# SyncE's wait ahead of a key unit's load: from ScalarE's copy and the last direct product to the first product read from the copy

## The chip, the cores and the metric

The kernel runs on one core of a Trainium2 chip. Its time is the device time of one execution in microseconds (us). Before the change the median of three runs is 694.32 us (693.97 to 694.38). A profile of one execution shows what each engine and the DMA did within its span; that execution took 693.89 us in all, 692.1 us of it the span.

## The reference

One decode step of a gated mix of two blocks, for a single token x of 512 numbers, all in float32:

```python
q = (x @ wq)                       # 32 heads of 128; 8 key/value heads, 4 query heads share one
scores = einsum("bhqd,bhkd->bhqk", q, k) * (Dh ** -0.5)
p = softmax(scores, axis=-1)       # over 32768 cached positions
a = einsum("bhqk,bhkd->bhqd", p, v) @ wo
b = (silu(x @ w1) * (x @ w3)) @ w2 # the MLP, 1792 wide
g = sigmoid((x * gate_w).sum(-1))
return g * a + (1 - g) * b
```

The key cache and the value cache are 8 x 32768 x 128 float32 each, 134 MB apiece. Nearly all bytes that the kernel reads are these two.

## The kernel before, in words

**Units.** The key cache is read in 16 units of 128 partitions x 16384 float32 (8.4 MB), four units to a window of two key/value heads. The value cache is read in 16 units of the same size. A unit's number is called t for keys; values run four units behind keys (`LAG = 4`).

**Buffers.** Two large SBUF buffers hold one unit each: `big_a` and `big_b` (keys `A0`, `A1`, `B0`, `B1` for their halves, called regions z = 0 and z = 1). Key units 0 and 2 go into `big_b`, units 1 and 3 into `big_a`; after these the MLP weights w1 and w3 and then the value units use `big_b`, and every later key unit goes into `big_a`. So from unit 4 on a key unit's load has to wait until the unit before it has been read out of `big_a`.

**Reading a key unit.** `set_aside` (L318) lets ScalarE copy three quarters of region z = 1 into a third buffer, `aside`, so that the large buffer comes free sooner. `scores` works in eight parts, (z, c) with z = 0, 1 and c = 0 to 3. For each part VectorE transposes 128 x 2048 numbers into one of two small buffers (L346; `kt`, of which one lies beside `aside` and bears that name in the profile), and TensorE multiplies the result with the query window (L330, `scores_part`). The parts (0, 0) to (0, 3) and (1, 0) are read from the large buffer itself, and (1, 1), (1, 2), (1, 3) from ScalarE's copy. Unit 3 is an exception: its part (1, 0) is copied as well (L320, into `extra`, a free corner of `big_b`), so that `big_a` is read by z = 0 and ScalarE alone, and a one-element VectorE copy `mark2` (L352) marks the end of the transposes of z = 0.

**Values.** `load_values` (L413) loads a value unit into `big_b` once TensorE has finished the products of the previous one (`values_all`, L432).

**What sets the order.** Each engine has its own list of operations, written in program order. `Program.add` works out the waits: an operation that writes a buffer waits for the buffer's writer and readers on other engines. VectorE's transposes hand over to TensorE by a semaphore that is counted down (a credit) and so have no running count of their own; whoever depends on one waits instead for the TensorE product that took the credit (`via`), a count on the semaphore `PE`. A wait that is implied by another one is left out: each operation carries the counts known to be reached when it is done (`after`). An operation with two waits gets a separate wait instruction first (L110) and has the second on the instruction itself.

SyncE issues all large loads through one queue (q1), in this order in the steady part: key unit, value unit, key unit, value unit. Before the change a key unit's load waits for two counts: ScalarE's, for the copy of the previous unit in that buffer, and TensorE's, for its product of part (1, 0). Unit 4's load waits for ScalarE's copy to `extra` and for VectorE's mark. Unit 1's load waits for the query products.

**The steps around it.** After each fourth unit, scores are turned (L368), reduced to a maximum by VectorE (L379 to L391) and put through the exponential by ScalarE (L398). At the end come the last value units, wo and w2, outside of the loops.

Of the kernel before, what the change touches and what calls it, by code (L numbers as in the profile page):

```python
# [23 lines left out]
class Program:  # L24
# [16 lines left out]
            self.sems[name] = self.sem(name)  # L41
        return self.sems[name]

    def add(self, eng, fn, reads=(), writes=(), over=(), inc=None, by=1, credit=None, credits=(), loop=False, also=None):

        op = Op(eng, fn, credits, loop)
        clock = self.clock[eng]
        for c, _ in credits:
            for k, v in c.after.items():
                clock[k] = max(clock.get(k, 0), v)  # L50
        deps = {}
        for k in reads:
            assert k in self.writer, k
            deps[self.writer[k]] = True
        for k in (*writes, *over):
            if k in self.writer:
                deps[self.writer[k]] = True
            for r in self.readers.get(k, ()):
                deps.setdefault(r, False)
        need = {}  # L60
        taken = {c for c, _ in credits}
        for d, data in deps.items():
            if d in taken or (d.eng == eng and (eng == "PE" or not data)):
                continue
            if d.done is None:
                d = d.via
                if d is None or d.eng == eng:
                    assert d is not None
                    continue
            k, v = d.done  # L70
            if clock.get(k, 0) < v:
                need[k] = max(need.get(k, 0), v)
        for k, v in sorted(need.items(), key=lambda kv: -self.by[kv].index):
            if clock.get(k, 0) >= v:
                continue
            assert not loop, (fn, k, v)
            op.waits.append((k, v))
            for a, b in self.by[k, v].after.items():
                clock[a] = max(clock.get(a, 0), b)
        op.index = len(self.by)  # L80
        op.after = dict(clock)
        if credit:
            op.inc = (credit, by)
        elif inc is None and by == 0:
            op.inc = None
        else:
            s = inc or eng
            self.count[s] = self.count.get(s, 0) + by
            op.inc, op.done = (s, by), (s, self.count[s])
            op.after[s] = self.count[s]  # L90
            self.by[op.done] = op
        for c, _ in credits:
            c.via = op
        for k in reads:
            self.readers.setdefault(k, []).append(op)
        for k in writes:
            self.writer[k], self.readers[k] = op, []
        if also:
            self.writer[also] = op
        self.ops[eng].append(op)  # L100
        return op
# [15 lines left out]
def kernel(  # L117
# [13 lines left out]
    nc = tc.nc  # L131
# [16 lines left out]
    LAG = 4  # L148
# [12 lines left out]
    def sbuf(name, *shape):  # L161
        return nc.alloc_sbuf_tensor(name, [P, *shape], F32)[:]

    big = [sbuf("big_a", 2 * R), sbuf("big_b", 2 * R)]
# [22 lines left out]

    lanes = [0]

    def load(dst, src, writes, over=()):  # L190
        lanes[0] += 1
        lane = f"load{lanes[0] % 9}"
        return pr.add(
            "SP", lambda: nc.sync.dma_start(dst, src), writes=writes, over=[*over, lane], inc=lane, by=16, also=lane,  # L194
        )

    def region(b, z):
        return big[b][:, z * R:(z + 1) * R]
# [26 lines left out]
    for src, dst, view, axes in (  # L225
# [11 lines left out]
            reads=[src], writes=[dst])  # L237
# [6 lines left out]
    def clear(**kw):  # L244
        pe(zeros,
           reads=["acc"], writes=["s"], **kw)
# [15 lines left out]
    for c in range(NC):  # L262
# [19 lines left out]
        reads=["gate0"], writes=["gate1"])  # L282
# [4 lines left out]
    for b in range(2):  # L287
        qt = kt[b][:, 0:512]
        dve(lambda b=b, qt=qt: V.transpose(qt, rows[b]), reads=[f"row{b}"], writes=[f"kt{b}"])
        for j in range(4):  # L290
            w, u = divmod(4 * b + j, 2)
            src = qt[32 * j:32 * j + 32, :].rearrange("p (q c x) -> p x c q", q=4, c=4)[:, 0]
            for e in range(2):
                r, o = 2 * u + e, 16 + 8 * e + 4 * u
                dst = win[32 * r:32 * r + 32, w, :, o:o + 4]
# [5 lines left out]
    kd = k_cache.rearrange("a (w u) s d -> w (a u s d)", u=2).rearrange("w (p m r) -> w m p r", p=P, m=4)  # L301
    vd = v_cache.rearrange("a h (e p n) d -> (a h) e p (n d)", e=2, p=P)

    def where(t):
        return 1 if t in (0, 2) else 0

    def load_keys(t):
        b = where(t)
        load(big[b], kd[t // 4, t % 4], ["AB"[b] + str(z) for z in range(2)])

# [3 lines left out]
    def set_aside(t):  # L316
        src, key = region(where(t), 1).rearrange("p (n r) -> p n r", n=NB), "AB"[where(t)] + "1"
        act(lambda: A.copy(spare, src[:, :, 32:128]), reads=[key], writes=["wo"])  # L318
        if t == LAG - 1:
            act(lambda: A.copy(extra, src[:, :, 0:32]), reads=[key], writes=["extra"], over=["B1"])  # L320

    def window(t, z):
        return act(
            lambda: A.copy(winc, win[:, t // 4, :, 16 - 16 * z:48 - 16 * z]),  # L324
            reads=[("win", t // 4, r) for r in range(4)], writes=["winc"], credit="windows",
        )

    def scores_part(c):
        for g in range(4):
            ins = T.matmul(  # L330
                ps_s[32 * g:32 * g + 32, :], winc[:, c, :], kt[c % 2][:, 512 * g:512 * g + 512],
                start=False, stop=False, skip_group_check=True,
            )
        return ins

    def scores(t, z, win_op):
        kin = region(where(t), z).rearrange("p (n c j) -> p c n j", c=4, j=32)
        ks = []
        for c in range(4):
            src, key = kin[:, c], "AB"[where(t)] + str(z)  # L340
            if (z, c) >= (1, 1):
                src, key = spare[:, :, 32 * (c - 1):32 * (c - 1) + 32], "wo"
            elif z == 1 and t == LAG - 1:
                src, key = extra, "extra"
            dst = kt[c % 2].rearrange("p (n i) -> p n i", i=32)
            k = dve(lambda d=dst, s=src: V.transpose(d, s), reads=[key], writes=[f"kt{c % 2}"], credit="keys")  # L346
            pe(lambda c=c: scores_part(c), reads=[f"kt{c % 2}", "winc"], writes=["s"], loop=True,
               credits=((win_op, 1), (k, 1)) if c == 0 else ((k, 1),))
            ks.append(k)

        if t == LAG - 1 and z == 0:
            done = dve(lambda: V.tensor_copy(mark2, ones[:, 0:1]), reads=["ones"], writes=["mark2"])  # L352
            for k in ks:
                k.via = done

    def scores_out(t):
        o = act(
            lambda: A.copy(sb[:, :, :, t % 4], ps_s.rearrange("p (n i) -> p n i", i=32)),  # L358
            reads=["s"], writes=[("sb", t % 4)], credit="scores",
        )  # L360
        return o
# [80 lines left out]
    def own(s):  # L442
        h, e = divmod(s, 2)
        dve(lambda: V.tensor_tensor(
            tmp[:, e], ps_o.rearrange("p (b d) -> p b d", b=4), own_b.unsqueeze(2).to_broadcast([P, 4, P]), op=ALU.mult,
        ), reads=["o", "own_b"], writes=[f"tmp{e}"])
        if e == 1:
            dve(lambda: V.tensor_reduce(red[h], tmp.rearrange("p e b d -> p d (e b)"), axis=AX.X, op=ALU.add),  # L448
                reads=["tmp0", "tmp1"], writes=[("red", h)])


    def load_hidden():
        for z, t in enumerate((w1, w3)):
            load(big[1][:, z * NC * F:(z + 1) * NC * F], t.rearrange("(p c) f -> p (c f)", c=NC), [f"B{z}"])
# [28 lines left out]
    def store(e, src, key, inc):  # L483
        i, q = (0, nc.scalar) if e == "ACT" else (1, nc.sync)
        pr.add(e, lambda: q.dma_start(outs[2 * i:2 * i + 2, :], src[31 + 64 * i:33 + 64 * i, :]),
               reads=[key], writes=[("out", i)], inc=inc, by=16)

    load_keys(0)
    vals = {}
    first = window(0, 0)  # L490
    for t in range(NH):
        v = t - LAG
        set_aside(t)
        scores(t, 0, first)
        scores(t, 1, window(t, 1))
        out_op = ((scores_out(t), 1),)
        if v < 0:
            clear(loop=True, credits=out_op)
        if t == LAG - 1:
            load_hidden()  # L500
        if t + 1 < NH:
            load_keys(t + 1)
            first = window(t + 1, 0)
        if v >= 1:
            own(v - 1)
        if t % 4 == 3:
            turn(v >= 0, out_op if v >= 0 else ())
        if v >= 0:
            values_loop(vals.pop(v), weights(v), () if t % 4 == 3 else out_op)
            clear(loop=True)  # L510
        if t == LAG - 1:
            hidden_products()
        if v + 1 >= 0 and t + 1 < NH:
            vals[v + 1] = load_values(v + 1)

        if t % 4 == 3:
            softmax(t // 4)
        if t % 4 == 0 and t > 0:
            total(t // 4 - 1)
        if t == LAG:  # L520
            hidden()
# [175 lines left out]
    a, b, c, d = flips  # L697
# [67 lines left out]
```

## Time and profile before

| what | us |
|---|---|
| median of three runs | 694.32 (693.97 to 694.38) |
| the profiled execution | 693.89 |
| its span | 692.1 |
| TensorE busy | 388.3 |
| VectorE busy | 370.1 |
| ScalarE busy | 134.7 |
| SyncE's separate waits, for ScalarE's copy | 195.7, 14 of them |
| SyncE's waits for TensorE's score products | 124.2, 17 of them |

How to read the rows: the page's first part gives each engine's busy time and share of the span. A line of the table by stretches gives the stretch, its length, busy time of PE (TensorE), PEld (its weight loads), DVE (VectorE), ACT (ScalarE) and POOL (GpSimd) with instruction counts, the granted TensorE clock, the mean busy share of the 16 DMA engines, and GB/s. A line of the timeline gives start, duration, engine, line of the kernel, operation, output and input, and in square brackets the idle time before it and what ended it; SPq is SyncE's queue, and its lines are issues of transfers. A line of the waits gives who waited, for whom, the total, the count and the longest. A line of the DMA issues ends with the time from issue to landing; where it was asked for a short stretch, it is that of the one transfer issued there.

### The profile page before, as it was taken

To read this page: it belongs to the slowest core of one execution; us is meant where nothing else is said; L and a number is where in the kernel's file an instruction comes from. 1 tells how busy PE (TensorE), PEld (TensorE's weight loads), DVE (VectorE), ACT (ScalarE), POOL (GpSimd) and SP (SyncE) were. 2 spreads that over 40 slices of the span, in tenths; PEclk is the share of its full clock that TensorE was granted. 3 is DMA by queue.
4 is the path that set the end of the run, shared out by engine and by line. 5 is a ranking of instruction groups with operands and counts; after the bars stand their busy time and mean duration, and the time that the engine had idled before them with its cause. 6 is when DMAs were issued, how large, how long until landed. Compare 5 with 4: busy or idle time off the path is not lost. (4 is left out here: it accounts for less than half of the span.)

```text
span 692.1 us, 5789 instructions
## 1 busy us (share of the span) xinstructions
PE 388.3 (56%) x2448; PEld 95.3 (14%) x2448; DVE 370.1 (53%) x259; ACT 134.7 (19%) x113; POOL 2.8 (0%) x15
## 2 busy tenths in 40 slices
PE   1537677566473636565564646364563646564457
PEld 0101111201010101201010101101010101211112
DVE  1049998493725637493826537492816547600701
ACT  0143323222303131220303131220303031100000
POOL 1000000000000000000000000000000000000000
PEclk9969999968686966778695779788697879865789
DMA  9999999999999999999999999999999999999996
GB/s 394 444 432 424 428 424 432 449 439 432 424 432 424 443 447 432 428 428 428 432 443 443 428 428 428 428 443 447 432 424 428 428 436 439 421 451 425 422 429 287
DMA packets 6213, 296.35 MB, mean 428 GB/s; under 512 B 694, under 2 KB 698, under 8 KB 1084
## 3 DMA queue, kind: packets, MB, share of 16 engines
q1 hardware_dynamic: 6196, 296.23, 99.1%
q8 instruction: 6, 0.10, 0.1%
q14 instruction: 3, 0.02, 0.0%
q10 hardware_dynamic: 8, 0.01, 0.0%
HBM read 296.23 MB, written 0.00 MB: 428 GB/s over the span
## 5 line engine op out<-in xcount | busy, mean ns | idle before, releaser
L346 DVE STREAM_TRANSPOSE aside<-big_a 128x2048 f32<-128x2048 f32 x41 | 94.4, 2302 | 184.3 <-DMA big_a<-in_A_k_cache_dram 184.3
L330 PE MATMUL ps<-aside,winc 128*32 128x512 f32 x512 | 89.4, 776 | 168.0 <-PEq L703 167.2
L330 PE MATMUL ps<-kt,winc 128*32 128x512 f32 x512 | 89.0, 772 | 49.1 <-PEq L703 49.1
L318 ACT COPY aside<-big_a 128x6144 f32<-128x6144 f32 x14 | 74.4, 5313 | 171.2 <-DMA big_a<-in_A_k_cache_dram 171.2
L432 PE MATMUL ps<-big_b,pv 128*32 128x512 f32 x768 | 94.9, 650 | 17.4 <-PEq L703 17.4
L346 DVE STREAM_TRANSPOSE kt<-aside 128x2048 f32<-128x2048 f32 x32 | 72.7, 2273 | 0.0
L346 DVE STREAM_TRANSPOSE kt<-big_a 128x2048 f32<-128x2048 f32 x28 | 63.5, 2269 | 0.0
L330 PEld LDWEIGHTS ps<-aside,winc 128*32 128x32 f32 x512 | 13.1, 120 | 236.6 <-issue 236.6
L358 ACT COPY sb<-ps 128x512 f32<-128x512 f32 x16 | 17.1, 1071 | 136.5 <-PE ps L330 136.5
L432 PEld LDWEIGHTS ps<-big_b,pv 128*32 128x32 f32 x768 | 27.7, 119 | 85.0 <-issue 85.0
L346 DVE STREAM_TRANSPOSE aside<-aside 128x2048 f32<-128x2048 f32 x16 | 36.3, 2269 | 0.0
L587 PE MATMUL ps<-big_b,probs 128*32 128x512 f32 x128 | 19.1, 756 | 21.1 <-DMA big_b<-in_A_v_cache_dram 21.1
L330 PEld LDWEIGHTS ps<-kt,winc 128*32 128x32 f32 x512 | 13.1, 120 | 125.4 <-issue 125.4
L596 DVE TENSOR_SCALAR red<-ps,own_b 128x128 f32<-128x128 f32 x2 | 0.7, 350 | 52.7 <-PE ps L587 52.7
L324 ACT COPY winc<-win 128x128 f32<-128x128 f32 x32 | 9.8, 307 | 77.9 <-PE ps L330 77.9
L587 PE MATMUL ps<-big_a,probs 128*32 128x512 f32 x128 | 18.1, 730 | 7.6 <-DMA big_a<-in_A_v_cache_dram 7.6
L346 DVE STREAM_TRANSPOSE aside<-big_b 128x2048 f32<-128x2048 f32 x7 | 16.0, 2291 | 11.0 <-DMA big_b<-in_A_k_cache_dram 11.0
L641 PE MATMUL ps<-win,ones 128*128 128x512 f32 (+1 forms) x40 | 21.8, 631 | 0.0
L242 PE MATMUL ps<-acc 128*128 128x512 f32 x34 | 20.0, 670 | 2.5 <-POOL acc L213 1.5
L379 DVE TENSOR_REDUCE mt<-turned 128x8 f32<-128x2048 f32 x4 | 9.2, 2292 | 20.3 <-PE turned L368 20.3
L405 DVE TENSOR_REDUCE sums<-probs 128x8 f32<-128x2048 f32 x4 | 15.3, 3834 | 2.1 <-ACT probs L398 2.1
L268 PE MATMUL turned<-big_a,xp 128*32 128x512 f32 x64 | 8.6, 699 | 12.0 <-DMA big_a<-in_A_wq_dram 12.0
(94 smaller groups left out, 186.9 us busy)
## 6 DMA issues: line engine op xcount, KB each, us to landing
big_b<-in_A_v_cache_dram SPq DMA_DIRECT2D x2, 4096.0 KB, 25.8
big_b<-in_B_w_dram SPq DMA_DIRECT2D x2, 3584.0 KB, 20.8
aside<-in_A_wo_dram SPq DMA_DIRECT2D x1, 4096.0 KB, 29.4
big_a<-in_A_wo_dram SPq DMA_DIRECT2D x1, 4096.0 KB, 20.4
big_a<-in_B_w_dram SPq DMA_DIRECT2D x2, 1024.0 KB, 23.5
big_a<-in_B_w_dram SPq DMA_DIRECT2D x1, 768.0 KB, 26.0
big_a<-in_B_w_dram SPq DMA_DIRECT2D x1, 512.0 KB, 26.7
big_a<-in_B_w_dram SPq DMA_DIRECT2D x1, 256.0 KB, 26.9
```

The costliest lines, as they stand in the source:

```text
L242: return T.matmul(ps_s, acc[:, 0:P], acc, start=True, stop=False, skip_group_check=True)
L268: ins = T.matmul(pf[b][32 * j:32 * j + 32, :], xp[:, c, :], t[:, o:o + REP * DH], start=(c == 0), stop=(c == NC - 1),)
L318: act(lambda: A.copy(spare, src[:, :, 32:128]), reads=[key], writes=["wo"])
L324: lambda: A.copy(winc, win[:, t // 4, :, 16 - 16 * z:48 - 16 * z]),
L330: ins = T.matmul(ps_s[32 * g:32 * g + 32, :], winc[:, c, :], kt[c % 2][:, 512 * g:512 * g + 512], start=False, stop=False, skip_group_chec ...
L346: k = dve(lambda d=dst, s=src: V.transpose(d, s), reads=[key], writes=[f"kt{c % 2}"], credit="keys")
L358: lambda: A.copy(sb[:, :, :, t % 4], ps_s.rearrange("p (n i) -> p n i", i=32)),
L379: dve(lambda: V.tensor_reduce(mt[:, 0:8], turned.rearrange("p (n q) -> p q n", q=8), axis=AX.X, op=ALU.max), reads=banks, writes=["mt"])
L405: dve(lambda: V.tensor_reduce(sums[:, 8 * w:8 * w + 8].rearrange("p (u q) -> p u q", u=2), probs[:, :, 0:1024].rearrange("p u (n q) -> p u ...
L432: ins = T.matmul(ps_o[32 * t:32 * t + 32, :], pv[:, o:o + 32], big[1][:, n * P:(n + 4) * P], start=((z, g) == (0, 0)), stop=((z, g) == (1, ...
L587: ins = T.matmul(ps_o[32 * t:32 * t + 32, :], prob[u][:, o:o + 32], vt[:, n * P:(n + 4) * P], start=((e, z, g) == (0, 0, 0)), stop=((e, z, ...
L641: return T.matmul(bank[:, 0:n], ones, win.rearrange("p w c n -> p (w c n)")[:, 0:n], start=True, stop=True)
```

## The change

A key unit's load gets an added dependency, `behind`: the VectorE transpose of part (1, 1), which is the first that reads ScalarE's copy. Through `via` it becomes a wait for TensorE's product of part (1, 1). Since that transpose comes after ScalarE's copy, the wait for ScalarE is implied by it and is left out, and so is the earlier count on TensorE. Which unit's part it is: the unit that occupied the same buffer, that is the second last one for units 2 and 3 (`read[-2:-1]`) and the last one from unit 4 on (`read[-1:]`). For unit 1 the slice is empty and nothing is added. In the changed order the loads of units 2, 3 and 5 to 15 wait for TensorE alone, and unit 4's for VectorE's mark and TensorE. All engines keep their instructions and their order; loads that do not go through `load_keys` keep their waits. In the changed file the lines stand two to four further down (L194 becomes L196, L330 becomes L332, L346 becomes L348).

```diff
-    def add(self, eng, fn, ..., loop=False, also=None):
+    def add(self, eng, fn, ..., loop=False, also=None, behind=()):
...
+        for d in behind:
+            deps[d] = True
...
-    def load(dst, src, writes, over=()):
+    def load(dst, src, writes, over=(), behind=()):
...
-            "SP", lambda: nc.sync.dma_start(dst, src), writes=writes, over=[*over, lane], inc=lane, by=16, also=lane,
+            "SP", lambda: nc.sync.dma_start(dst, src), writes=writes, over=[*over, lane], inc=lane, by=16, also=lane, behind=behind,
...
-    def load_keys(t):
+    def load_keys(t, behind=()):
         b = where(t)
-        load(big[b], kd[t // 4, t % 4], ["AB"[b] + str(z) for z in range(2)])
+        load(big[b], kd[t // 4, t % 4], ["AB"[b] + str(z) for z in range(2)], behind=behind)
...
             ks.append(k)
+            if (z, c) == (1, 1):
+                read.append(k)
...
-    vals = {}
+    vals, read = {}, []
...
         if t + 1 < NH:
-            load_keys(t + 1)
+            load_keys(t + 1, read[-1:] if t + 1 >= LAG else read[-2:-1])
             first = window(t + 1, 0)
```

More of the change, by code (lines that the diff above doesn't have):

```diff
@@ L42, in semaphore, with add @@
         return self.sems[name]
-    def add(self, eng, fn, reads=(), writes=(), over=(), inc=None, by=1, credit=None, credits=(), loop=False, also=None):
+    def add(self, eng, fn, reads=(), writes=(), over=(), inc=None, by=1, credit=None, credits=(), loop=False, also=None, behind=()):
         op = Op(eng, fn, credits, loop)
```

## The prediction

> **What bounds the kernel now.** I read the busy shares and the DMA row of the page first, then the DMA shares over four long stretches, then the landings of the key units as ScalarE sees them.
>
> ```profile
> PE 388.3 (56%) x2448; PEld 95.3 (14%) x2448; DVE 370.1 (53%) x259; ACT 134.7 (19%) x113; POOL 2.8 (0%) x15
> DMA  9999999999999999999999999999999999999996
> q1 hardware_dynamic: 6196, 296.23, 99.1%
> 0.00:43.30 43.30, 11.62 (x72) 3.74 (x72) 4.39 (x13) 6.14 (x21) 2.81 (x15) 0.92 0.97 412
> 43.30:137.90 94.60, 65.05 (x376) 15.86 (x376) 77.31 (x46) 31.99 (x21) 0.00 (x0) 0.95 1.00 433
> 137.90:563.90 426.00, 236.38 (x1462) 52.50 (x1462) 237.70 (x135) 87.42 (x64) 0.00 (x0) 0.76 1.00 434
> 563.90:690.00 126.10, 75.30 (x538) 23.19 (x538) 50.69 (x65) 9.12 (x7) 0.00 (x0) 0.78 0.97 418
> 292.71 5.31 ACT L318 COPY aside<-big_a 128x6144 f32<-128x6144 f32 x1 [3.44 <-DMA big_a<-in_A_k_cache_dram]
> 331.41 5.31 ACT L318 COPY aside<-big_a 128x6144 f32<-128x6144 f32 x1 [17.94 <-DMA big_a<-in_A_k_cache_dram]
> 370.11 5.31 ACT L318 COPY aside<-big_a 128x6144 f32<-128x6144 f32 x1 [17.44 <-DMA big_a<-in_A_k_cache_dram]
> 408.81 5.31 ACT L318 COPY aside<-big_a 128x6144 f32<-128x6144 f32 x1 [17.11 <-DMA big_a<-in_A_k_cache_dram]
> 447.82 5.31 ACT L318 COPY aside<-big_a 128x6144 f32<-128x6144 f32 x1 [7.51 <-DMA big_a<-in_A_k_cache_dram]
> ```
>
> No compute engine is busy for more than 56% of the span; queue q1, on which SyncE puts every large load, fills 99.1% of the 16 DMA engines. From 43.3 to 563.9 us the DMA share is 1.00 at 433 to 434 GB/s. A key unit's landing is the moment ScalarE's copy of it starts: 292.71, 331.41, 370.11, 408.81, always 38.70 us apart, and between two lie one key and one value transfer of equal size, so 19.35 us each. (The last gap is 39.01; I return to it.) While the queue is never empty the end moves by nothing: a load issued later only waits less behind its predecessor. So the question for this change is by how much each load is issued ahead of its predecessor's landing (its lead), and what lead a load needs.
>
> **The change: what is removed.** SyncE now makes two waits ahead of a key unit's load: one on ScalarE's copy (L110, the separate instruction) and one on TensorE (on the load itself, L194).
>
> ```profile
> SPq L110 <- ACT aside L318: 195.7, 14, 16.6
> SPq L194 <- PE ps L330: 124.2, 17, 16.8
> ```
>
> The 195.7 us are no cost: SyncE has nothing else to do, the copy is over 5.31 us after landing (292.71 + 5.31 = 298.02), and the load goes at 305.12. Removing the separate wait gives nothing, since the later wait, on TensorE, stays. What could it be worth at most? One instruction for each load, 0.04 us or so by the time between a product's end and the issue (below), spent where the lead hides it.
>
> **What is moved.** The 14 loads of units 2 to 15 now wait for the product of part (z, c) = (1, 1) instead of (1, 0). One steady unit shows both:
>
> ```profile
> 286.06 0.33 SPq L413 DMA_DIRECT2D big_b<-in_A_v_cache_dram  x1
> big_b<-in_A_v_cache_dram SPq DMA_DIRECT2D x1, 26.0
> 304.01 1.07 PE L330 MATMUL ps<-aside,winc 128*32 128x512 f32 x8 [1.13 <-PEq L703]
> 305.12 0.33 SPq L194 DMA_DIRECT2D big_a<-in_A_k_cache_dram  x1
> 306.20 1.93 PE L330 MATMUL ps<-kt,winc 128*32 128x512 f32 x8 [1.13 <-PEq L703]
> 322.08 0.33 SPq L413 DMA_DIRECT2D big_b<-in_A_v_cache_dram  x1
> 344.96 1.07 PE L330 MATMUL ps<-kt,winc 128*32 128x512 f32 x8 [1.13 <-PEq L703]
> big_a<-in_A_k_cache_dram SPq DMA_DIRECT2D x14, 26.3
> ```
>
> Here (1, 0) ends at 305.08 and the load goes 0.04 later. (1, 1) ends at 306.20 + 1.93 = 308.13, so the load would go at 308.18, 3.06 us later. The value load ahead of it, issued at 286.06, takes 26.0 us to landing: 312.06. The lead falls from 6.94 to 3.88 us. The 1.93 us is a product at half clock; the next unit's takes 1.07, so its load goes at 346.08, and its predecessor lands midway between 331.41 and 370.11, at 350.76: lead 4.68. Of the 11 loads issued in units 4 to 14, three see the slow product (those of units 5 and 11 are the other two) and eight the fast one:
>
> ```profile
> 190.10 1.94 PE L330 MATMUL ps<-kt,winc 128*32 128x512 f32 x8 [1.13 <-PEq L703]
> 422.30 1.93 PE L330 MATMUL ps<-kt,winc 128*32 128x512 f32 x8 [1.13 <-PEq L703]
> 56.79 1.06 PE L330 MATMUL ps<-kt,winc 128*32 128x512 f32 x8 [1.13 <-PEq L703]
> 62.65 2.31 DVE L346 STREAM_TRANSPOSE aside<-big_a 128x2048 f32<-128x2048 f32 x1 [1.62 <-DMA big_a<-in_A_k_cache_dram]
> ```
>
> For unit 2's load, behind unit 0's product: 56.79 + 1.06 + 0.05 = 57.90 against a landing at 62.65, lead 4.75. Unit 3's load stands alike.
>
> Unit 4's load is the odd one. Unit 3 is copied whole out of its buffer, so today the load goes after VectorE's mark at 110.16, when only z = 0 has been transposed. The change keeps that wait and adds (1, 1) of unit 3, two products further on:
>
> ```profile
> 94.34 0.33 SPq L194 DMA_DIRECT2D big_b<-in_B_w_dram  x1
> big_b<-in_B_w_dram SPq DMA_DIRECT2D x1, 3584.0 KB, 24.0
> 110.16 0.11 DVE L352 COPY mark<-ones 128x1 f32<-128x1 f32 x1
> 110.30 0.33 SPq L194 DMA_DIRECT2D big_a<-in_A_k_cache_dram  x1
> 114.83 1.06 PE L330 MATMUL ps<-kt,winc 128*32 128x512 f32 x8 [1.13 <-PEq L703]
> ```
>
> New issue: 114.83 + 1.06 + 0.05 = 115.94, which is 5.64 later. Its predecessor, the second MLP weight load, lands at 94.34 + 24.0 = 118.34. The lead falls from 8.04 to 2.40: the least of all. Behind it on SyncE's queue stands only the first value load, which goes at 130.60 after the MLP products and does not feel it. In the steady stage the value load behind the key load of 305.12 goes at 322.08, on its own wait for TensorE's value products; a key load 3 us later does not push it. Unit 1's load and all loads after unit 15 keep their waits. TensorE, VectorE and ScalarE run the same instructions; nobody waits for a key load but the next unit's readers, and they wait for its landing.
>
> **What lead is needed.** The trace has no large load with so short a lead, so I bound the need from both sides.
>
> ```profile
> 0.93 0.40 SPq L194 DMA_DIRECT2D big_a<-in_A_wq_dram  x1
> big_a<-in_A_wq_dram SPq DMA_DIRECT2D x1, 21.9
> 130.60 0.33 SPq L413 DMA_DIRECT2D big_b<-in_A_v_cache_dram  x1
> big_b<-in_A_v_cache_dram SPq DMA_DIRECT2D x1, 26.6
> 150.71 0.33 SPq L194 DMA_DIRECT2D big_a<-in_A_k_cache_dram  x1
> 137.91 5.31 ACT L318 COPY aside<-big_a 128x6144 f32<-128x6144 f32 x1 [3.24 <-DMA big_a<-in_A_k_cache_dram]
> 176.61 5.31 ACT L318 COPY aside<-big_a 128x6144 f32<-128x6144 f32 x1 [15.25 <-DMA big_a<-in_A_k_cache_dram]
> ```
>
> Below: the very first load, of a unit's size, finds all engines empty and lands 21.9 us after issue, 19.35 of which is transfer; starting cold costs 2.55 us. Above: the load at 150.71 has the shortest lead among the unit loads today, 130.60 + 26.6 - 150.71 = 6.49, and its unit lands 38.70 after the one before: no loss. So a load needs at most 6.49, and I take 2.55, because an engine that has emptied is in the state of that first row, and one that has not loses nothing at all. Loss at need L: (L - 2.40) once, 3 x (L - 3.88), 8 x (L - 4.68) and two more near 4.75 (each where positive). At 2.55 that is 0.15 us; at 6.49 it is 4.1 + 7.8 + 14.5 + 3.5 = 29.9 us, the far end.
>
> The Trainium skill, "DMA: Bandwidth & Descriptors", section "Anatomy of one DMA — SWDGE (gpsimd) path", gives a fixed cost of about 2.0 us for each DMA beside its bytes. This was fitted on the GpSimd path; by it the need is an estimated 2.0, below every new lead, and the sum is 0 instead of 0.15. The row of the first load, 2.55, decides.
>
> **The sum.** Removed wait 0, eleven steady and two early loads 0, unit 4's load +0.15: span 692.1 to 692.25. The profiled run took 693.89 us, 1.8 outside its span; the median of the runs shown is 694.32, 0.43 above it. I carry the 0.15 to the median: 694.5 us.
>
> **Rivals.**
> *The queue runs dry (slower).* If a load needs more than 3.79 us from issue to full flow, unit 4's load alone costs 1.39 us (0.2% of 694.32, about what a measurement of this kernel can tell from no change), and from 3.88 on the three half-clock units add theirs. At L = 4.35, say, 1.95 + 3 x 0.47 = 3.4 us, 697.7 us. For it: no row shows a lead between 2.55 and 6.49 beside a running transfer. Against it: the cold start, with nothing to hide behind, took 2.55. The same page of the Trainium skill, "Latency and other measured facts", has HBM access at 0.2 us on average and 2 us at high load; that this would be paid at a hand-over is a possibility that no row here shows, and 2.55 + 1.8 is where my example of 4.35 would lie by it.
>
> *The stream loses its two hiccups, or more (faster).* The trace's stream is late twice: unit 4 lands 137.91 - 118.34 = 19.57 after its predecessor instead of 19.35, and the gap of 39.01 is 0.31 too long; in that stretch an instruction fetch lies among the loads:
>
> ```profile
> q14 instruction: 1, 0.01, 0.7%
> ```
>
> With fewer wait instructions both could vanish: 0.5 us, 693.8 us, which is still no change. For a gain over 1.39 us the DMA engines would have to run above 434 GB/s, or the start or the end to shrink, and the change touches none of these.
>
> *The waits do not move.* If the added dependency were already covered, the load would go as now and the time stay 694.3. Against it: in the changed order each of these loads lists TensorE's wait without ScalarE's (unit 4's: VectorE's and TensorE's).
>
> **How the numbers follow.** Forecast, with the third rival and the hiccups inside it, 0.80: between 692.9 and 695.7. Running dry 0.15, faster beyond 0.2% by something I do not see 0.05. So faster 0.05, same 0.80, slower 0.15. The range goes from 693.6 (both hiccups gone and 0.2 for the runs' spread) to 696.0, which takes in unit 4's loss up to L = 4.
>
> **What would show it.** In the changed profile: unit 4's load at about 115.9 and landed about 22 us later; steady key loads about 2.2 us later than now, 3.1 at half clock; their median time to landing near 24 instead of 26.3; the separate wait on ScalarE's copy listed once (ahead of the first value load into that buffer) instead of 14 times; key landings still 38.70 apart. I am wrong if that distance grows, or if unit 4 lands after 139.3.

## The result and the profile after

The changed kernel is slower: 698.24 us, median of 11 runs (696.12 to 701.99), against 694.10 us (693.87 to 694.38, 11 runs) before, a ratio of 1.0061 with a 95% interval of 1.0041 to 1.0080. Both the loss and the spread are new: the runs before lie within 0.5 us, those after over 6 us. The profiled execution is one of the shorter ones: 696.29 us, span 694.3, which is 2.2 us over the span before.

The page's engine and DMA rows of the changed kernel hardly differ from before:

```profile
PE 390.3 (56%) x2448; PEld 96.5 (14%) x2448; DVE 370.1 (53%) x259; ACT 134.6 (19%) x113; POOL 2.8 (0%) x15
DMA  9999999999999999999999999999999999999997
q1 hardware_dynamic: 6196, 296.23, 99.0%
```

SyncE's waits of the changed kernel show that the change did what it says. The separate wait on ScalarE's copy is there once instead of 14 times, and the wait for score products has taken over its time:

```profile
SPq L196 <- PE ps L332: 339.5, 18, 26.1
SPq L112 <- ACT aside L320: 15.7, 1, 15.7
SPq L112 <- DVE mark L356: 15.6, 1, 15.6
```

The timeline of the changed kernel around unit 4's load, with the landings of unit 3 (VectorE's start at 101.67) and of units 4 to 6 (ScalarE's starts):

```profile
94.67 0.33 SPq L196 DMA_DIRECT2D big_b<-in_B_w_dram  x1
101.67 2.31 DVE L348 STREAM_TRANSPOSE aside<-big_a 128x2048 f32<-128x2048 f32 x1 [1.68 <-DMA big_a<-in_A_k_cache_dram]
115.15 1.07 PE L332 MATMUL ps<-kt,winc 128*32 128x512 f32 x8 [1.13 <-PEq L707]
116.27 0.33 SPq L196 DMA_DIRECT2D big_a<-in_A_k_cache_dram  x1
139.24 5.31 ACT L320 COPY aside<-big_a 128x6144 f32<-128x6144 f32 x1 [4.24 <-DMA big_a<-in_A_k_cache_dram]
178.24 5.31 ACT L320 COPY aside<-big_a 128x6144 f32<-128x6144 f32 x1 [16.46 <-DMA big_a<-in_A_k_cache_dram]
216.96 5.31 ACT L320 COPY aside<-big_a 128x6144 f32<-128x6144 f32 x1 [17.46 <-DMA big_a<-in_A_k_cache_dram]
```

And its DMA issues (the second weight load, unit 4's load, and the median of all 14 key loads into `big_a`), with the time to landing last:

```profile
big_b<-in_B_w_dram SPq DMA_DIRECT2D x1, 3584.0 KB, 24.0
big_a<-in_A_k_cache_dram SPq DMA_DIRECT2D x1, 23.0
big_a<-in_A_k_cache_dram SPq DMA_DIRECT2D x14, 24.0
```

Unit 4's load goes at 116.27, ahead of a landing at 94.67 + 24.0 = 118.67: lead 2.40, as forecast. But its unit lands 20.57 after that, not 19.35. Measured from unit 3 to unit 4, the distance is 139.24 - 101.67 = 37.57 us; two weight loads and a key unit need 36.37 when the queue is never empty (all but unit 4, below). So 1.2 us are lost there. From unit 4 to 5 it is 39.00 instead of 38.70, after which 38.72.

The DMA packets across that hand-over show where they go. On each of the 16 engines a load ends with a packet of under 512 B, and the next load begins with one of 64 KB. The lines are those of the DMA view: packets started in a stretch, bytes, rate, and the small ones among them. Before (115.94 to 116.89 us), 14 engines end the weight load and begin unit 4's at once:

```profile
DMA packets 29, 0.95 MB, mean 996 GB/s; under 512 B 14, under 2 KB 14, under 8 KB 14
```

After, from the issue of unit 4's load on (116.27 to 117.22), 14 engines end and nothing follows:

```profile
DMA packets 15, 0.03 MB, mean 30 GB/s; under 512 B 14, under 2 KB 14, under 8 KB 14
```

The new load's first packet starts at 117.23, 0.96 us after its issue; the very first load of the kernel, before the change, needed 1.03 us (issue at 0.93, first packet at 1.96). The 15th engine ends at 117.31, and the last one at 118.18; its end is the landing, which is signalled at 118.67. So the lead of 2.40 was one ahead of the last engine alone, and 14 of 16 had already run empty. The 16 first packets then take 2.93 x 1.03 = 3.0 us each (DMA share times length of the stretch in which they start, columns as in the prediction's stretches), where a packet of the steady stream takes 19.35 / 8 = 2.42:

```profile
117.22:118.25 1.03, 0.96 (x9) 0.19 (x8) 1.03 (x1) 0.00 (x0) 0.00 (x0) 1.00 2.93 1018
```

That hits the last engine too: it had not run empty, and its first packet takes 3.1 us. The rest of the 1.2 us, 0.4, is an instruction fetch: the engine that carries 16 KB of it at 132.48 ends its share at 138.73, the other 15 by 138.30. The load was issued before its predecessor had landed, and the stream still has a hole.

### The profile page after: what moved, and what is told of

The parts are those of the page before. It is cut to its first block, busy times and chain, and to the rows that moved or that the text cites. A ratio compares the mean times of both kernels' runs of the same rounds, so it can differ in the third digit from the quotient of the medians.

```text
span 694.3 us, 5776 instructions
## 1 busy us (share of the span) xinstructions
PE 390.3 (56%) x2448; PEld 96.5 (14%) x2448; DVE 370.1 (53%) x259; ACT 134.6 (19%) x113; POOL 2.8 (0%) x15
## 5 line engine op out<-in xcount | busy, mean ns | idle before, releaser
L348 DVE STREAM_TRANSPOSE aside<-big_a 128x2048 f32<-128x2048 f32 x41 | 94.4, 2304 | 188.8 <-DMA big_a<-in_A_k_cache_dram 188.8
L332 PE MATMUL ps<-aside,winc 128*32 128x512 f32 x512 | 90.8, 787 | 172.3 <-PEq L707 171.4
L332 PE MATMUL ps<-kt,winc 128*32 128x512 f32 x512 | 88.5, 769 | 48.1 <-PEq L707 48.1
L348 DVE STREAM_TRANSPOSE kt<-aside 128x2048 f32<-128x2048 f32 x32 | 72.7, 2272 | 0.0
L348 DVE STREAM_TRANSPOSE kt<-big_a 128x2048 f32<-128x2048 f32 x28 | 63.6, 2270 | 0.0
L332 PEld LDWEIGHTS ps<-aside,winc 128*32 128x32 f32 x512 | 13.1, 121 | 240.2 <-issue 240.2
L348 DVE STREAM_TRANSPOSE aside<-aside 128x2048 f32<-128x2048 f32 x16 | 36.3, 2270 | 0.0
L332 PEld LDWEIGHTS ps<-kt,winc 128*32 128x32 f32 x512 | 13.0, 120 | 125.7 <-issue 125.7
L348 DVE STREAM_TRANSPOSE aside<-big_b 128x2048 f32<-128x2048 f32 x7 | 16.1, 2297 | 11.2 <-DMA big_b<-in_A_k_cache_dram 11.2
```

The lines of the kernel that those rows point to most:

```text
L332: ins = T.matmul(ps_s[32 * g:32 * g + 32, :], winc[:, c, :], kt[c % 2][:, 512 * g:512 * g + 512], start=False, stop=False, skip_group_chec ...
```

## The experiments

Theory A: a hand-over from one load to the next needs a longer lead than a cold start showed, and each key load pays when its lead is short. Rival B: only unit 4's load is too late. Rival C: the loss comes with the removed separate wait, not with the later issue. In the kernels below the code line that differs from the changed kernel is given.

| kernel | us, median (range), runs | ratio to before (95%) |
|---|---|---|
| the changed kernel again | 699.20 (696.66 to 701.07), 6 | 1.0078 (1.0057 to 1.0098) |
| unit 4's load alone moved | 695.14 (695.08 to 696.19), 11 | 1.0018 (1.0009 to 1.0027) |
| all but unit 4's moved | 695.82 (694.57 to 699.92), 12 | 1.0034 (1.0020 to 1.0048) |
| behind part (1, 2) | 717.48 (715.90 to 719.48), 5 | 1.0333 (1.0320 to 1.0347) |
| one wait, old time | 694.12 (693.70 to 694.74), 11 | 1.0003 (0.9994 to 1.0012) |
| both waits, new time | 696.94 (696.20 to 697.70), 5 | 1.0043 (1.0029 to 1.0057) |
| two halves | 695.57 (695.49 to 697.11), 8 | 1.0024 (1.0013 to 1.0034) |
| units 2, 3 and 4 moved | 696.64 (695.70 to 697.56), 5 | 1.0033 (1.0020 to 1.0046) |
| units 5 to 15 moved | 696.12 (695.41 to 698.51), 6 | 1.0039 (1.0025 to 1.0052) |

The kernel before, run beside them, had medians of 693.95 to 694.05 us; a single execution of it beside three of the traced ones took 694.98.

**The changed kernel again.**

> The changed kernel once more, for the spread of its executions. Theory A (each hand-over from one load to the next needs more lead than the cold start showed, and every key load pays a part that differs from execution to execution): a median of 696 to 700 us and a spread of several us, with packets' hand-overs late at several units in the trace. Rival B (only unit 4's load is too late, a fixed loss): about 1.2 us over the kernel before, 695.5 us, with a spread like that of before, below 1 us.

The median of 699.2 and the spread of 4.4 us are A's; B, which had 695.5 us and a spread below 1, falls.

**Unit 4's load alone.**

```diff
-            load_keys(t + 1, read[-1:] if t + 1 >= LAG else read[-2:-1])
+            load_keys(t + 1, read[-1:] if t + 1 == LAG else ())
```

> Only unit 4's load gets the added dependency; the others wait as before the change. A: unit 4's share alone, 1.0 to 1.5 us over before (695.1 to 695.6 us), and the spread of the executions gone. B: the whole loss, the same median as the changed kernel. Rival C (the loss comes with the removed separate wait, not with the time of issue): no loss, 694.1 us.

1.1 us and little spread. The timeline has the loss in one place, 138.67 - 101.25 = 37.42 between units 3 and 4, and 38.71 from there on:

```profile
101.25 2.31 DVE L348 STREAM_TRANSPOSE aside<-big_a 128x2048 f32<-128x2048 f32 x1 [1.69 <-DMA big_a<-in_A_k_cache_dram]
138.67 5.31 ACT L320 COPY aside<-big_a 128x6144 f32<-128x6144 f32 x1 [4.08 <-DMA big_a<-in_A_k_cache_dram]
177.38 5.31 ACT L320 COPY aside<-big_a 128x6144 f32<-128x6144 f32 x1 [16.12 <-DMA big_a<-in_A_k_cache_dram]
```

C would have to lay the whole 1.1 us on the one merged wait that is left; the kernels with one wait at the old time and with both at the new test that.

**All but unit 4's load.**

```diff
-            load_keys(t + 1, read[-1:] if t + 1 >= LAG else read[-2:-1])
+            load_keys(t + 1, () if t + 1 == LAG else read[-1:] if t + 1 >= LAG else read[-2:-1])
```

> Unit 4's load waits as before the change; the loads of units 2, 3 and 5 to 15 have the added dependency. A: the loss less unit 4's share, 1 to 4 us over before (695 to 698 us), and the spread of several us still there; unit 4 lands 19.5 us after its predecessor as before. B: no loss, 694.1 to 694.3 us. C: the whole loss of the changed kernel.

1.8 us, with the spread. In the traced execution (695.53 us) unit 4 lands 137.84 - 101.47 = 36.37 after unit 3, nothing lost. Unit 7 lands 39.28 after unit 6 (254.54 - 215.26) instead of 38.70; of its 1.5 us of longer span most of the rest, 1.1 us, comes at a value load (see the last point of the section on the prediction):

```profile
101.47 2.31 DVE L348 STREAM_TRANSPOSE aside<-big_a 128x2048 f32<-128x2048 f32 x1 [1.70 <-DMA big_a<-in_A_k_cache_dram]
137.84 5.31 ACT L320 COPY aside<-big_a 128x6144 f32<-128x6144 f32 x1 [3.05 <-DMA big_a<-in_A_k_cache_dram]
215.26 5.31 ACT L320 COPY aside<-big_a 128x6144 f32<-128x6144 f32 x1 [17.30 <-DMA big_a<-in_A_k_cache_dram]
254.54 5.31 ACT L320 COPY aside<-big_a 128x6144 f32<-128x6144 f32 x1 [18.52 <-DMA big_a<-in_A_k_cache_dram]
```

**Behind part (1, 2).**

```diff
-            if (z, c) == (1, 1):
+            if (z, c) == (1, 2):
```

> The added dependency is the product of part (1, 2) instead of (1, 1): each load 2.2 us later still, its lead to the landing ahead of it about 2.4 us, as unit 4's was in the changed kernel. A: each of the 13 loads of units 2, 3 and 5 to 15 loses about 1.2 us as unit 4's did, unit 4's 3.4: some 19 us over before, about 713 us. B: unit 4's load alone, 3.4 us over before, 697.5 us. C: as the changed kernel, 698 us.

23.4 us, more than A's 19. Unit 2 lands 84.81 - 62.88 = 21.93 after unit 1 instead of 19.35, on the timeline (VectorE's first transposes of units 1 and 2):

```profile
62.88 2.31 DVE L348 STREAM_TRANSPOSE aside<-big_a 128x2048 f32<-128x2048 f32 x1 [1.63 <-DMA big_a<-in_A_k_cache_dram]
84.81 2.31 DVE L348 STREAM_TRANSPOSE aside<-big_b 128x2048 f32<-128x2048 f32 x1 [4.27 <-DMA big_b<-in_A_k_cache_dram]
```

Over the steady stretch (columns as in the prediction's stretches) the DMA share drops from 1.00 to 0.98 and the rate from 434 to 416 GB/s:

```profile
137.90:563.90 426.00, 221.83 (x1384) 51.05 (x1388) 233.05 (x133) 85.70 (x61) 0.00 (x0) 0.76 0.98 416
```

**One wait, at the old time.** VectorE's transpose of (1, 0) also waits for ScalarE's copy, so that the product of (1, 0) covers both readers; unit 4's load waits as before.

```diff
-            k = dve(..., reads=[key], ...)
+            k = dve(..., reads=[key, "wo"] if (z, c) == (1, 0) and t != LAG - 1 else [key], ...)
...
-            if (z, c) == (1, 1):
+            if (z, c) == (1, 0):
...
-            load_keys(t + 1, read[-1:] if t + 1 >= LAG else read[-2:-1])
+            load_keys(t + 1, () if t + 1 == LAG else read[-1:] if t + 1 >= LAG else read[-2:-1])
```

> One wait on SyncE as in the changed kernel, but at the old time: VectorE's transpose of part (1, 0) also waits for ScalarE's copy (long done by then), so that TensorE's product of (1, 0) covers both readers; unit 4's load waits as before the change. A (lead): the leads are those of before, 694.0 us, spread below 1 us. C (the removed separate wait): as the changed kernel, 696 to 700 us.

694.12 us: the single wait neither costs nor gains. Units land 38.70 us apart on the timeline:

```profile
292.71 5.31 ACT L320 COPY aside<-big_a 128x6144 f32<-128x6144 f32 x1 [5.58 <-DMA big_a<-in_A_k_cache_dram]
331.41 5.31 ACT L320 COPY aside<-big_a 128x6144 f32<-128x6144 f32 x1 [17.09 <-DMA big_a<-in_A_k_cache_dram]
```

And the key loads' median time to landing among its DMA issues is 26.3 us, as before the change:

```profile
big_a<-in_A_k_cache_dram SPq DMA_DIRECT2D x14, 26.3
```

**Both waits, at the new time.**

```diff
-        for k, v in sorted(need.items(), key=lambda kv: -self.by[kv].index):
+        for k, v in sorted(need.items(), key=lambda kv: self.by[kv].index if behind else -self.by[kv].index):
```

> The changed kernel with the separate waits on ScalarE's copy (and on the load's own semaphore, long reached) kept ahead of the wait for the product of (1, 1). A: the leads are those of the changed kernel or up to 0.1 us shorter, 696 to 700 us with a spread of several us. C: the loss goes, 694.1 us.

A separate instruction is back ahead of each load, though not as before the change: it waits for TensorE's product and ScalarE's copy together, and the load itself for the earlier load into its buffer, long landed. The load goes 0.06 us behind that instruction.

```profile
SPq L112 <- PE ps L332: 309.6, 14, 25.9
```

The loss stays, 3.0 us. Together with the kernel above this shows that the time of issue costs, and that one wait in place of two costs nothing by itself. It does not show that the waits have no share at all: the spread is 1.5 us where several were expected, and none of the five executions is above 697.7, while nine of the 17 of the changed kernel are above 698. The trace shows one of the places: TensorE's product of (1, 1) at half clock (1.93 us) ahead of unit 6's load, and 217.33 - 177.64 = 39.69 us between units 5 and 6:

```profile
177.64 5.31 ACT L320 COPY aside<-big_a 128x6144 f32<-128x6144 f32 x1 [15.38 <-DMA big_a<-in_A_k_cache_dram]
191.13 1.93 PE L332 MATMUL ps<-kt,winc 128*32 128x512 f32 x8 [1.13 <-PEq L707]
217.33 5.31 ACT L320 COPY aside<-big_a 128x6144 f32<-128x6144 f32 x1 [18.95 <-DMA big_a<-in_A_k_cache_dram]
```

**Two halves.**

```diff
-        load(big[b], kd[t // 4, t % 4], ["AB"[b] + str(z) for z in range(2)], behind=behind)
+        for z in range(2):
+            load(region(b, z), kd[t // 4, t % 4][:, z * R:(z + 1) * R], ["AB"[b] + str(z)], behind=behind if z else ())
```

> Each key unit is loaded in two halves: region z = 0 as soon as its own four parts are multiplied (about 4 us earlier than now), region z = 1 behind the product of (1, 1) as in the changed kernel. A: the queue never has less than 8 us of lead ahead of it, so the hand-over loss and the spread go; what is left is 0.06 us for each unit from the smaller pieces (two loads of 4 MB took 9.71 each in the trace before, a whole one 19.35): 695.1 us, spread below 1 us. C or any theory by which the wait for (1, 1) itself costs: 698 us as the changed kernel.

695.57 us: the wait for (1, 1) is there, the lead is long (12.8 us and more for each half of units 2 to 15 in its trace), and the loss goes down to 1.6 us, 0.5 more than the smaller pieces were to cost; the spread is 1.6 us where less than 1 was expected. It is no better version than the kernel before.

**Which loads carry the spread.** Single executions of the changed kernel were traced too:

> The changed kernel once more, for a trace. A: hand-overs to key units that take up to 1 us more than 19.35 at units which differ from one execution to the next, unit 4 always at about 20.4.

> The changed kernel again, for a trace of one of its long executions (699 us and more). Theory A1 (the loss is many short leads): a long execution shows more units whose hand-over takes more than 19.35 us, each by up to 1 us, most of them after products at half clock, where the lead is 3.8 us. Rival A2 (few large losses): one or two hand-overs with several us, at places where instructions are fetched (near 430, 600, 640 and 677 us).

> As again3: one more execution of the changed kernel for its trace.

> As again3: one more execution of the changed kernel for its trace.

They took 696.50, 696.11, 698.70 and 695.87 us. In the long one, `again4`, unit 2 lands 82.94 - 63.07 = 19.87 after unit 1 (0.5 over), and unit 4 lands 141.47 - 102.27 = 39.20 after unit 3 (2.8 over, where the other traces of the changed kernel have 0.95 to 1.5):

```profile
63.07 2.31 DVE L348 STREAM_TRANSPOSE aside<-big_a 128x2048 f32<-128x2048 f32 x1 [0.74 <-DMA big_a<-in_A_k_cache_dram]
82.94 2.31 DVE L348 STREAM_TRANSPOSE aside<-big_b 128x2048 f32<-128x2048 f32 x1 [2.21 <-DMA big_b<-in_A_k_cache_dram]
102.27 2.31 DVE L348 STREAM_TRANSPOSE aside<-big_a 128x2048 f32<-128x2048 f32 x1 [1.67 <-DMA big_a<-in_A_k_cache_dram]
141.47 5.31 ACT L320 COPY aside<-big_a 128x6144 f32<-128x6144 f32 x1 [5.86 <-DMA big_a<-in_A_k_cache_dram]
```

Unit 4's load is issued at 116.87 there. Fourteen engines begin it within 1.8 us; the other two do so only at 120.29 and 120.37, 3.4 and 3.5 us after the issue, and they are the last to end. Between 118.80 and 120.70 these two are the only packets of 64 KB that start:

```profile
DMA packets 3, 0.13 MB, mean 69 GB/s; under 512 B 1, under 2 KB 1, under 8 KB 1
```

Neither guess fits as it stands. Four other units lose 0.1 to 0.5 us each, as A1 has it, but 2.8 of the 4.8 us by which the span is longer lie at one hand-over, which is more than A1 said and not at a place that A2 named. The last two kernels separate the early loads from the steady ones:

```diff
-            load_keys(t + 1, read[-1:] if t + 1 >= LAG else read[-2:-1])
+            load_keys(t + 1, () if t + 1 > LAG else read[-1:] if t + 1 == LAG else read[-2:-1])   # units 2, 3, 4
+            load_keys(t + 1, read[-1:] if t + 1 > LAG else ())                                     # units 5 to 15
```

> The added dependency for the loads of units 2, 3 and 4 alone. If the long executions come from unit 4's load finding the DMA engines unsettled by the two short leads before it (in the longest traced execution it lost 2.83 us and unit 2's 0.52): a median of 696 to 697 us and single executions near 699. If they come from the eleven steady units: 695.2 us with a spread below 1.2 us, as with unit 4 alone.

> The added dependency for the loads of units 5 to 15 alone. If the long executions come from the steady units: a median of 695 to 697 us and single executions near 699. If they come from the early loads: 694.1 to 694.8 us, spread about 1 us.

Both lose, 2.7 and 2.1 us by their medians, and both spread, by 1.9 and 3.1 us; the sum of 4.8 is near the changed kernel's 4.1 to 5.1. So neither group alone carries it. In the early one's trace (697.56 us) unit 2 is late again, by 82.67 - 62.60 - 19.35 = 0.7 us, and again unit 4 pays more than alone: 140.38 - 102.03 = 38.35, 2.0 over.

```profile
62.60 2.31 DVE L348 STREAM_TRANSPOSE aside<-big_a 128x2048 f32<-128x2048 f32 x1 [0.74 <-DMA big_a<-in_A_k_cache_dram]
82.67 2.31 DVE L348 STREAM_TRANSPOSE aside<-big_b 128x2048 f32<-128x2048 f32 x1 [2.41 <-DMA big_b<-in_A_k_cache_dram]
102.03 2.31 DVE L348 STREAM_TRANSPOSE aside<-big_a 128x2048 f32<-128x2048 f32 x1 [1.70 <-DMA big_a<-in_A_k_cache_dram]
140.38 5.31 ACT L320 COPY aside<-big_a 128x6144 f32<-128x6144 f32 x1 [5.01 <-DMA big_a<-in_A_k_cache_dram]
```

**The price of a lead.** The key loads of units 2 to 15 in the traces of all kernels with whole key loads, before included, grouped by lead (from issue to the landing ahead of it); the loss is the distance between the two landings less 19.35 us:

| lead, us | loads | with over 0.1 us lost | mean loss, us | largest |
|---|---|---|---|---|
| under 2.2 | 5 | 5 | 2.55 | 3.32 |
| 2.2 to 2.6 | 12 | 11 | 1.48 | 2.83 |
| 2.6 to 3.3 | 5 | 4 | 0.79 | 1.67 |
| 3.7 to 4.1 | 19 | 9 | 0.29 | 1.00 |
| 4.1 to 5.6 | 99 | 2 | 0.01 | 0.24 |
| over 5.6 | 56 | 3 | 0.01 | 0.31 |

The three in the last row are the hiccups of the stream that the prediction named, in the kernel before and in the one with one wait at the old time. The need is no fixed number, since the engines neither end a load nor begin the next one at the same time: at 3.7 to 4.1, which is mostly where a half-clock product puts a steady load, every second one loses.

## Why the prediction was wrong, point by point

**What bounds the kernel: right.** The DMA stream does, and the time after is the time before plus the holes in it.

**The removed wait, worth nothing: right.** One wait at the old time gives 694.12 us; both waits at the new time lose 3.0.

**The moved issues: right.** Unit 4's load at 116.27 (115.94 forecast, in a stream that was 0.33 later from the start), lead 2.40; the median time to landing fell to 24.0 (24 forecast). Unit 4's own load landed 23.0 us after its issue, where about 22 was forecast; that belongs to the next point.

**The lead that is needed: wrong, and this is the step that failed.** I took the 2.55 us of the first load, "because an engine that has emptied is in the state of that first row, and one that has not loses nothing at all". The lead was reckoned to the landing, which is the end of the last engine. In the profiled execution 14 of the 16 engines had emptied before the first packet of unit 4's load, although that load was issued 2.40 us ahead; and the last engine, which had not, lost 0.7 us as well, by a first packet of 3.1 instead of 2.42 us. In the traces unit 4's load lost 0.95 to 2.83 us at a lead of 2.3 to 2.4 (2.40 in this execution), which makes the need 3.35 to 5.2 us; steady loads lost up to 1.0 us at 3.8 to 4.0, need up to 4.8. All within the two ends that I had set, 2.55 and 6.49, but not at the lower one. (The shortest lead before was unit 7's, 6.48 us, not that of the load at 150.71; nothing changes by it.) The term "unit 4's load +0.15" was 1.1 us alone (the kernel with that load alone), and the zeros of the other loads, together with what their move does to later loads, were 1.8 us (the kernel without it).

**The rival "the queue runs dry", given 0.15, is in the main what happened**, at the loads that it named and, as it did not say, at value loads too (last point). Its example, a need of 4.35 and 697.7 us, came 0.5 us from the measured 698.24. Part of that is luck: it has 1.95 us at unit 4's load, which cost 1.1 alone, and nothing at the value loads, and the executions of which 698.24 is the median differ by 6 us. The Trainium skill, "DMA: Bandwidth & Descriptors", section "Latency and other measured facts", has HBM access at 2 us at high load; the estimate by it, 2.55 + 1.8 = 4.35, came nearer than my row. That the extra time is HBM's latency is not shown: the first packets of unit 4's load start no later after the issue (0.96 us) than those of the first load (1.03).

**"Unit 4 lands after 139.3" and "that distance grows"** were named as what would show me wrong. The first was missed by a hair in the profiled execution (139.24) and met in `again4` (141.47); the second occurs at single units, not at every one.

**Not in any term: the spread, and a loss at a load with a long lead.** The first value load into `big_a` has the lead of before (6.9 us) and yet lands 0.3 to 1.5 us late in nine of the twelve traces with moved loads. Before, it goes at 576.34 and lands 26.3 us later, at 602.6, 38.7 after unit 15 (one value unit and itself). The timeline of before and its DMA issue:

```profile
563.93 5.31 ACT L318 COPY aside<-big_a 128x6144 f32<-128x6144 f32 x1 [18.00 <-DMA big_a<-in_A_k_cache_dram]
576.34 0.33 SPq L194 DMA_DIRECT2D big_a<-in_A_v_cache_dram  x1
```

```profile
big_a<-in_A_v_cache_dram SPq DMA_DIRECT2D x1, 26.3
```

In the changed kernel's `again` it lands at 577.65 + 27.8 = 605.45, 40.2 after unit 15. Its timeline, and its DMA issue with the fetch of 595 to 603 us:

```profile
565.24 5.31 ACT L320 COPY aside<-big_a 128x6144 f32<-128x6144 f32 x1 [17.94 <-DMA big_a<-in_A_k_cache_dram]
577.65 0.33 SPq L196 DMA_DIRECT2D big_a<-in_A_v_cache_dram  x1
```

```profile
big_a<-in_A_v_cache_dram SPq DMA_DIRECT2D x1, 27.8
q8 instruction: 1, 0.02, 0.8%
```

That instruction fetch on queue q8 is there in both kernels. It takes one DMA engine for 1.07 us, and that engine's next packet takes 2.91 us instead of 2.42. Before, the engine it falls on runs ahead of the others and ends its share of the value load at 601.73, the last one at 602.15: nothing is lost. In `again` the engine it falls on ends at 605.01, the other 15 by 603.30; from 603.40 to 605.20 only its small last packet is still to come:

```profile
DMA packets 29, 0.92 MB, mean 510 GB/s; under 512 B 1, under 2 KB 1, under 8 KB 1
```

So this loss is the fetch, on an engine that is no longer one of those ahead. That short leads are what puts the engines out of step fits the kernels (the load is not late in the traces of before and of one wait at the old time), but is not shown by itself. It is no small part: in the six traces of the changed kernel the distances between landings grew, in sum, by 0.5 to 1.2 us at the moved key loads (3.4 in `again4`) and by 0.7 to 1.7 us at value loads, whose waits were not changed. The executions of 699 us and more were timed and not traced; that they add up from the same two kinds of loss stays open.

## What to carry to other kernels

In a kernel that is bound by its DMA stream, moving a load's release later is free only while its lead stays where the trace has already shown no loss. Here that was above 5.6 us; from 4.1 to 5.6 two of 99 loads paid, and below 4.1 half of them or more. A lead is to be reckoned to the first engines that end, not to the landing, which is the last one's; and since the engines end and begin at different times, the price of a cold start is no measure for a hand-over between running transfers. Between two far ends, the cheap test is to move one load and look. And a wait that is long over by the time the load goes costs nothing, so merging it buys nothing; where one wait is wanted, let an earlier operation take over the dependency and keep the time of issue.

## What the runs showed of the hardware that I had not expected

A load issued 2.4 us before its predecessor landed still cost the stream about 1 us or more, where 2.55 us from issue to full flow, as at the cold start, would have cost 0.15. Fourteen of the 16 engines had ended their share before the new load's first packet, 0.96 us after its issue. An instruction fetch of 16 KB among the loads held one engine up by 1.07 us and its next packet by another 0.5, and whether that cost anything depended on how far ahead that engine was. Short leads do not add simply: in the two traces where unit 2's load had lost 0.5 to 0.7 us, unit 4's lost 2.0 to 2.8 instead of 0.95 to 1.5, some 35 us later. And the loss varies between executions of one kernel by 6 us (696.12 to 701.99), where the same kernel with long leads varies by 0.5.
